# A gated recurrence and a PReLU layer on one core: two kinds of sums moved from VectorE to TensorE, factors folded, and the hand-made instruction order replaced

## The chip, the core and the metric

The kernel runs on one core of a Trainium2 chip. The core has five engines with a queue of their own: TensorE (PE; the profile shows its weight loads apart, as PEld), VectorE (DVE), ScalarE (ACT), GpSimd (POOL) and SyncE (SP), which here issues all the DMA transfers. Each engine works through its queue in order and waits on semaphores for the others. The metric is device time in microseconds (us), the median of several executions; lower is better.

## The reference

An attention block with a gated complex state feeds a dense layer. For each of 4 batches and 8 heads, over 768 tokens with head size 48:

```python
mag = np.sqrt(a_re * a_re + a_im * a_im)
scale = np.minimum(mag, 0.999) / (mag + 1e-06)
a_re_n, a_im_n = (a_re * scale, a_im * scale)
for t in range(S):
    ar, ai = (a_re_n[:, :, t, :, None], a_im_n[:, :, t, :, None])
    new_re = ar * S_re - ai * S_im
    new_im = ar * S_im + ai * S_re
    kv = np.einsum('bhd,bhe->bhde', k[:, :, t], v[:, :, t])
    S_re, S_im = (new_re + kv, new_im)
    y[:, :, t] = np.einsum('bhd,bhde->bhe', q[:, :, t], S_re)
```

The outputs, as 3072 tokens of 384 numbers, go through `h = x @ w_in` (384 to 2048), `g = max(h, 0) + alpha * min(h, 0)` and `g @ w_out` (2048 to 384). All is float32.

## The kernel before

**Units.** The 768 tokens of a batch are six units of 128, so there are 24 units, 0 to 23. A unit (`unit`) first turns queries and keys by the accumulated phase of the gates (L742, L744, on DVE), and then makes six doubling steps (L797, one DVE instruction of 96x1024 each), between which PE forms the scores of a level (L759, tile `ps_lv`) and DVE or ACT masks them (L782, L773). After the steps its keys are transposed (L868, `ps_kt`), ACT copies them beside the unit's decays in tile `T` (L870, L871), PE multiplies keys by values (L880, `ps_kv`), and the state is carried on in two halves: ACT scales the old state (L916, eight instructions, one a head) and DVE adds `ps_kv` to it (L918). PE makes the outputs from scores (L900) and from the old state (L930), ACT copies them out (L944) and two DMAs write them to DRAM (`ysc`, L949).

**Gates.** Before a unit can begin, its gates must be there. `gates` works in nine groups: group 0 has one unit, group 1 two, groups 2 to 8 three units each. ACT squares the real and the imaginary part (L263 to L267; L299 to L303 for group 0), DVE adds the squares (L269; L305), ACT and DVE make the reciprocal root and the normalised gate (L272 to L291; L310 to L323, L363), and DVE makes the decays (L380). From them a tree of ever shorter products (L396) makes the decays of whole spans, and one DMA writes all to DRAM (`decs`, L401). Then come the phases: products of unit complex numbers in several passes (L416, L418, L477, L507, L510), and two DMAs (`phs`, L512). The units load them again as `PP` (L665) and `T` (L672).

**The dense layer.** It works on ten groups of tokens, m = 0 to 9: groups 0 and 1 have one unit each, the others two. `xT` is loaded from `ysc` (L962) when the group's units are out; `features` multiplies by `w_in` (L978, `ps_h`), ACT and DVE make the PReLU (L985, L987), and `outputs` multiplies by `w_out` (L997, `ps_o`). A last group of units is done with fewer products (L1097, L1172). The weights arrive as float64 and are turned into float32 on the way (L588 to L600).

**The order.** The body is written as tasks, Python generators that yield before each instruction. `ORDER` is a string with one letter a step: it says which task goes on next, and so fixes the order of every engine's queue and of the DMAs on SP. The numbers in `yield DVE(...)` do nothing in this program. In the kernel before, the decay tree is part of the gates' task, and a unit's transposes, state and outputs are one task in a fixed sequence.

**What is where at the start.** PE's first matmul is that of unit 0's first level. The first features (m = 0) need the outputs of unit 0; from then on PE has the units and the dense layer at once.

Of the kernel before, what the change touches and what calls it, by code (L numbers as in the profile page):

```python
# [15 lines left out]
PSUM = bass.MemoryType.PSUM  # L16
DRAM = bass.MemoryType.DRAM

P = 128
# [11 lines left out]
    "AAJMMAABAJAAAAAAAAAAAAAAAAAAAAMMMBJMAAAAAAAAAAKANAOAAAABAAANAAAKANNNABAMAJNBKOAKBOOKAABMAKABAAALOAAB"  # L31
    "LAKNOLNAALBOLANNAALBBLAAKBAKBBAKABABKMAAKBAAOAABAAAAAABABBABAAABAOOABABMANAAAAAAABAAAKBABNABBNBNOBOC"
    "BOCBJNNBLBOJBBOONBBNBBOCBBPBCBPPJLJMJCLKBNBCMBCJBPLBPCBOPPJCPBBBPOBPPBBNBPBBNNBBCPPMLPBLBBPLKBPKBCCC"
    "PLOKBKBPKBBBBCBPKCOOPKBPPPCPBPBCBPPPPBBPBCBBPBBPBBPBPCBPMPBCCBCBPNBKLCCNLCNPCPOCOJDCNDPPPJCOJNNCCCNJ"
    "OCNOOLCNOPCNKOMNNCPQPDJCQDLCDNQPPDQQQLCDQDKQQMCLNDQDOKPQQMODQLOOJQJDKQJDOLCQnOJOLDDJQNJOQLQLOOoLoDDC"
    "QLoQRQoLQQLQooooQQCoQDKNJooooRoMQoQCRCCoooooQoRDQQQCODDCONNCooRQRLoDCLRoMoLoCRRLCoooooCJoRDKCRKooooo"
    "RCDoRQLCDLCoooCoRKoOLCDJCQDCCoLDCRRDDCooooooLCQCooCLCoCoCoLCLCCCLCRCCLCKOCRCRLoCooCRRRCRRoRRCoCRCQQC"
    "CRCQCCoRKCRQRQQCQOORRoRCCQCCooRRCNQDoLoDLoNoDNoooNDoEDNNoEOJoDJRJDRLoooooDDoLDRRRLDRRLRDNDNEJDJSDDRo"
    "oJDESDEDSRDRJESSnJSoLESDoLoLODJSSJDSDLLTSDJoELoooooSSSDLoLooooJSSoDDDoSEDLoooSToSoJooJSSSDoSSDSSoooo"
    "ooSTSDETooooTToSEEoEDoooooSDToSEDTSESSSSDooLDTLoooLEEDSLToLSLoooooDLELoTJDSSSDoooooTTSDSESSSLoDooooo"  # L40
    "SEEDTLLoTKoooooDDDToTEJLDDDDoooooTEUJTDKoDoooKTToDoLoToooTLoUoDJoTLToooToEJoDonooToDEoDTKoUoDJooToUo"
    "EoEUTUEoETEDDDJTooUooDoUUoDooToToTTDoLoLoULoLDULLoooUUoDoLooooDoULoLoELooooLoUULoTLUTLJoooooFUEUoETT"
    "TUUUUTTTUooooTToUETUUFEoUEooooEoUVoUEoooooVVKJJUUEUUEUUoFooLEFLoUoLEUFJVUELoVJoUJooooVJEoFVEJEVoEUoo"
    "oUUUEVoEUoLoVVLEoooEoLEoVEJooooJVEWoFEnVVLoVELoLoooEoKVVEoELVEoJFooooJWoVoVFooWLooLVVEEWoLWVoLWVEFJV"
    "VVJEooVoVoooEKoWKoJEoooVEWWooVWoVoEFWVVVEVVEWELWEELooFEELoWLEoEoLoWWLVLoWEEEEVLLooooooLWEWLEoLEFELEK"
    "FFVVVooWooLooVVVVVFFFVLXKEoEWooooooEWWEEWWJoWWJoooWoEJWoWJoFJWoEWFFWWWWoEoELoLEoJoLoEoFXEooooFooooXo"
    "ooooKXWXLXFWoXoGGXLoXooooJWoLXoLWoFWXoXWFXWoFWXFWWoWXoXFFoFLoXoGFJFnGooooXXoJFoFLoLXXXXLGFLoooooXLFX"
    "XXoGoLFGFLoooooooFXoooGFoJoYJXoJFoJXFGKoooXFYFXoXFYJFooooGXXXYoYXLYFooLXFYFKoLoYoYLXXFZLFXLoXYXFLoXX"
    "XoooYXoFGLGFYYLoYGoFJoYFYJoooFoFZoLFoJoYJGKooooFJGYFYLooYYYLoJYYZGLLFoooooZLoFGYZYZoYZYKJFZZooooYFoZ"
    "YoYFGZYYFYFFYYFZFLFZFFLoYLoooZLooLoFFFFFYFZLFZYYYLFoZLYYFLYoooFZYLaZFLoFoooZZZZoYZZLZoGYFFLLoooZoZGo"  # L50
    "LGoFZJoZFFFGJoooooFooZFFZZFZZZGLoonoFLooLaoFoLoooaJoLoZoaJGoLZooaJaGoaoHoLZZLaaZoHGGoGZGZGGaZLGaLooo"
    "ooaZGaLoaJoZaZaooooGJoHaooHGoooaoaGLaHoooLoGLaaJaHoaJaaJoooooHoGbaoaGHoooaoGaobbJKHoaGaoaoaGaaHoLKoG"
    "JoboLGobLGoLGoooGbLoHGHbLboJbHoGJLaoLbbGLooooGoGHobLGaLaHbLGbabLaabaaGoLaooooLGbboGoGHbGooooJbGbGGKo"
    "bbboJobJbGGbcbbJobGGoooboGcbooooGbGoHbGbGcbbbLGcGLoooGbLcGHcGGJoboJcoLJGGGobLGccLGoobKcbLobHLbobbLoc"
    "obHoGHGdbLGHooooccocGoJoJHoooLcocdJooLconJHLoooocLcHoccccoccLGoJdcGGooocodHocHoHdHoHcGGGcoooGooocGGc"
    "GccccodGLLoooGcodooooLoddJoooLocdoLoIHIoHLdooooLHooLHdcoLdcoLdcLocJHcocddoHoHooKcoooILdocoLHoIHdcdLH"
    "LddoIKdooooJdoIddJoddKdHoHooodoHdoIoHedHHodeHIdddodoHLeHLoLoIHodLHoHLHeIHoLdLoooeeJHeHLoLdddHoooeeoH"
    "JHdedHLoJooooeIoLIeLeoeJddoLHoooLeeoLoHdIHeodJoHIHoooeeoJeeeeoeJeoeIJeoenJHIHoooeJIoeooHeHoHfeeoeHfe"
    "eoLLHoHHJHoHHeHoLfeoLILJHHHHofLooooofeLHfeHfLeHKoeIeLoKffLeHoooooefHeoeLgIIfogJLooooIoooffofoHJILooo"
    "ooHLffoJIoJfHHoooooKHofofJooLfffffofKoJgooHofgIoooggoIHIofofHIoIIoofoHKfooHofogfffoffggoLHLoLogoLoHI"  # L60
    "oLgoooILofnoIfgLgLgLfffoLggJoLgfKoooofooooIgLogfooLfIfofggggggogoohgogIhhLJJJIIhIooooogogoIIoogggggg"
    "oLILogoJIoJgIohJgIILgIgooohLIIgoJgIoIghILhIoIghILoLhhIooooIoIhIoJoLihILJooohhohLoLohLohoooLioJIIoLho"
    "LoJiJooohohooJhhiohhihJhihnoIIIhIoIIhIIIIooohIoIhIioIhihhhhhIihoLihLLLohhhLIIIIIiooooLohhiILiIoLiILo"
    "hLoooiiIoLohihohoLIoooILiIiLoLiiiiiioJioJioIIiIoooioiojoioIiiijIiiJooLojLoJoIoJoLjoooiLoIioLojIjiiiI"
    "jiiooooojjooooLojLiiJoooojLopoLjojiiLoooJjoLoojjJLojLLoooooJojLojooJjjjjjJojjJopjojookkkoojojooojjkj"
    "jojjokLkoLkLokJokoLokLoLoookLjooLjkJkokLLokkLoooLokooooLojjjLokjkjojkjjkojkkLlkookkopkJokJpoookokook"
    "oklkkkkLkLoookJlooLoLolooJokJopoJoLllJklnkLllokoooooklolokooollkkLLLolkoololoooJoLloJoLoooLlmlololoo"
    "oloLoLlooolLmooomololloolpmooolomlomopoomoomomoooomooomoollllllmmomoolomomoooolmoonoolllmmomlmomlmol"
    "lomomoooooooomLooLooooLoLoooLoooooooLoqLoooLooLomLooooLooLooLomLoooooooopooooomoooomoooooooooooooooo"
    "oooooooomomomoomoomomoooomomomoqlmqlmqmmmqqmqoooooqqoqoooooqoqqoqooqoqqooqoqqoqoqooqooqqoooooqoqqoqo"  # L70
    "ooooooooooqoooqoooqqoqqoqooooooooooqqooqoooooqqoqqoqooqoqooqoqqoqqqqqqqqoooooooooooqoqqoqoqooqooqooq"
    "oqoqooqoqoqoooqqqoqqonoooooooooooooooqooqqoqoqqoqqooooooooooooqqoqoqoooqooooooooooooqqqooqooqoooqoqq"
    "oqooooooooqqoooooooooqoooooooooooqooqoooqqoooqoqqqoqooooooooqoqoooqoqooooqqoqqoqooqoqooqqqoqoqqqqqqq"
    "ooooqoooooooqoqqoqooqqqoqoqooooooooooooqqqqqqoqqoooooooooooooooooqqqqoqqoqqooooooooooooooooooqoqqqoq"
    "oqoooooooooooooooooqqooooooooooooqoooqoqoooqoqqoqqoooooooooooqqqooooooqoqqoqqooqoqooqoqqqqqooooooooo"
    "ooqoqqoqooqoqooqqoqqqqqqqqqqqqqqqqqqqqqqqqq")


class Ring:

    def __init__(self, n):
        self.n = n

    def put(self, event, i=None):
        pass


class Plan:

    LETTERS = "ABCDEFGHIJKLMNOPQRSTUVWXYZabcdefghijklmnopqrstuvwxyz0123456789"  # L90
# [12 lines left out]

@with_exitstack
def kernel(
# [123 lines left out]
    def gates(g, b, c0, c1):  # L229
# [111 lines left out]
        def by_place(z):  # L341
            return z.rearrange("p (n m i) -> p m n i", m=L // 2, i=2)

# [917 lines left out]
```

## Time and profile before

| | |
|---|---|
| median of 3 runs | 823.86 us (821.32, 823.86, 829.38) |
| the profiled execution | 820.38 us, its span 818.6 us |
| busy in the span: PE | 681.1 us (83%) |
| DVE | 693.9 us (85%) |
| ACT | 520.3 us (64%) |
| POOL | 222.2 us (27%) |
| DMA | 130.99 MB, mean 160 GB/s |
| first matmul | at 54.1 us |
| first features of m = 0, 1, 2, 3 (L978) | at 120.1, 184.1, 220.3, 266.2 us |

The busy times add up to far more than the span, since the engines work side by side. What counts is which of them waits for which at each stage; the prediction shows the profile by stage.

### The profile page before, as it was taken

The numbers are of one execution on the slowest core, as the hardware profiler recorded it, in microseconds if no ns is written. First come the engines' busy times: TensorE is split into PE (matmuls) and PEld (weight loads), VectorE is DVE, ScalarE is ACT, GpSimd is POOL, SyncE is SP. The second block draws the span as 40 slices with busy tenths as digits, with TensorE's granted clock in tenths as the row PEclk, the third lists the DMA queues.
The fourth block names the chain that finished last, engine by engine and source line by source line (L and its number), as shares of the span: only waits on it lengthen the run. The fifth ranks groups of instructions, "written<-read, shape, count | busy, mean of one in ns | idle before, by whom it ended". The sixth has DMA issues, their size and how long they took to land.

```text
span 818.6 us, 27870 instructions
## 1 busy us (share of the span) xinstructions
PE 681.1 (83%) x11680; PEld 539.0 (66%) x11680; DVE 693.9 (85%) x1191; ACT 520.3 (64%) x1307; POOL 222.2 (27%) x293
## 2 busy tenths in 40 slices
PE   0003128659998999999999999999999999999997
PEld 0003126537776777767777777777777777899997
DVE  5999999999989899999999989998787775456574
ACT  8777998669666777876876697555756544312121
POOL 7231343051604310531245054003200000233342
PEclk9999659979999999999999999999999999999999
DMA  8594895593689589738865867787566622101000
GB/s 242 176 294 128 266 296 158 177 253 101 182 235 197 140 194 272 174 90 279 195 168 141 253 160 180 223 197 184 117 182 134 153 77 56 44 1 40 1 21 20
DMA packets 186598, 130.99 MB, mean 160 GB/s; under 512 B 74728, under 2 KB 176872, under 8 KB 186088
## 3 DMA queue, kind: packets, MB, share of 16 engines
q1 hardware_dynamic: 186472, 129.20, 59.3%
q8 instruction: 92, 1.51, 0.8%
q14 instruction: 34, 0.28, 0.1%
HBM read 100.82 MB, written 35.71 MB: 167 GB/s over the span
## 4 chain that ended last, share of the span: by engine, by line
PE 65%; DVE 14%; DMA 10%; ACT 4%; SPq 2%; issue 2%; POOL 1%; DVEq 0%; ACTq 0%; POOLq 0%
PE ps_o L997 19%; PE ps_h L978 18%; PE ps_m L1172 7%; PE ps_lv L759 5%; PE ps_y L1097 4%; PE ps_h L1097 4%; PE ps_y L900 3%; DVE KQ L797 2%; PE ps_kv L880 2%; PE ps_y L930 2%; DMA VL<-in_v_dram 2%; DVE gate L507 2%; PE ps_kt L868 1%; DVE gate L416 1%; DMA T<-decs 1%
## 5 line engine op out<-in xcount | busy, mean ns | idle before, releaser
L978 PE MATMUL ps_h<-xT,w_in_sb 128*128 128x256 f32 (+1 forms) x960 | 227.0, 369 | 2.1 <-DVE w_in_sb L600 1.6
L997 PE MATMUL ps_o<-w_out_sb,g_sb 128*128 128x384 f32 x576 | 222.1, 501 | 4.8 <-DVE g_sb L987 4.7
L978 PEld LDWEIGHTS ps_h<-xT,w_in_sb 128*128 128x128 f32 x960 | 170.9, 195 | 51.3 <-DVE w_in_sb L600 2.2
L797 DVE TENSOR_TENSOR KQ<-KQ,T 96x1024 f32<-96x1024 f32 x120 | 148.4, 1237 | 25.8 <-PE ps_lv L759 19.2
L997 PEld LDWEIGHTS ps_o<-w_out_sb,g_sb 128*128 128x128 f32 x576 | 102.5, 191 | 44.9 <-DVE g_sb L987 6.5
L985 ACT ACTIVATE g_sb<-ps_h 128x256 f32<-128x256 f32 (+1 forms) x160 | 57.9, 362 | 73.0 <-PE ps_h L978 72.2
L759 PE MATMUL ps_lv<-WQ 96*32 96x32 f32 x2304 | 34.4, 203 | 83.6 <-DVE WQ L742 70.2
L759 PEld LDWEIGHTS ps_lv<-WQ 96*32 96x32 f32 x2304 | 26.3, 116 | 105.9 <-DVE WQ L742 71.0
L916 ACT ACTIVATE St<-St,T 96x48 f32<-96x48 f32 x352 | 84.0, 325 | 4.6 <-DVE St L918 4.3
L987 DVE SCALAR_TENSOR_TENSOR g_sb<-g_sb,al,ps_h 128x256 f32<-128x256 f32 (+1 forms) x160 | 71.3, 446 | 13.7 <-ACT g_sb L985 13.1
L1160 POOL TENSOR_TENSOR sums<-g_sb 128x128 f32<-128x128 f32 x48 | 21.8, 475 | 185.5 <-DMA VL<-in_v_dram 110.6
L416 POOL TENSOR_TENSOR gate<-gate 128x72 f32<-128x72 f32 x42 | 34.5, 822 | 133.7 <-ACT gate L446 130.9
L596 POOL TENSOR_SCALAR top<-top 128x768 f32<-128x768 f32 x16 | 44.1, 2755 | 74.6 <-ACT top L588 63.2
L820 ACT COPY WQ<-KQ 96x1024 f32<-96x1024 f32 x48 | 50.0, 1041 | 18.9 <-DVE KQ L797 18.3
L416 DVE TENSOR_TENSOR gate<-gate 128x576 f32<-128x576 f32 (+5 forms) x84 | 50.7, 604 | 1.1
L900 PE MATMUL ps_y<-A,VL 64*48 64x64 f32 x2304 | 41.9, 220 | 4.4 <-issue 4.3
L900 PEld LDWEIGHTS ps_y<-A,VL 64*48 64x48 f32 x2304 | 39.0, 122 | 6.8 <-issue 6.7
L507 DVE TENSOR_TENSOR gate<-gate 128x1152 f32<-128x1152 f32 (+2 forms) x36 | 42.8, 1220 | 0.8 <-POOL gate L492 0.7
L1135 ACT ACTIVATE rl<-g_sb 128x256 f32<-128x256 f32 x24 | 10.0, 416 | 50.0 <-DVE g_sb L1128 50.0
L773 ACT ACTIVATE A<-ps_lv,columns 128x64 f32<-128x64 f32 x144 | 37.4, 336 | 6.2 <-PE ps_lv L759 5.9
L836 ACT COPY W<-KQ 96x512 f32<-96x512 f32 x48 | 30.8, 641 | 16.2 <-DVE KQ L797 8.7
L759 PE MATMUL ps_lv<-KQ,W 96*32 96x32 f32 x1536 | 24.7, 204 | 18.5 <-ACT W L836 17.4
(168 smaller groups left out, 1355.7 us busy)
## 6 DMA issues: line engine op xcount, KB each, us to landing
T<-decs SPq DMA_DIRECT2D x48, 384.0 KB
PP<-phs SPq DMA_DIRECT2D x24, 387.0 KB
KQ<-in_q_dram SPq DMA_DIRECT2D x48, 192.0 KB
decs<-gate SPq DMA_DIRECT2D x7, 1152.0 KB
phs<-gate SPq DMA_DIRECT2D x14, 576.0 KB
KQ<-in_k_dram SPq DMA_DIRECT2D x40, 192.0 KB
vsc<-in_v_dram SPq DMA_DIRECT2D x48, 144.0 KB
VL<-vsc SPq DMA_DIRECT2D x48, 144.0 KB
```

What stands on the lines that cost most here:

```text
L416: on(4 * k).tensor_tensor(out=m, in0=w[:, 1::-1].unsqueeze(2).to_broadcast([P, 2, 2, k]), in1=pairs_of(u), op=ALU.mult)
L507: TT(out=m[:, a], in0=U5[:, 1 + a], in1=turned(off3, o)[:, a].unsqueeze(1).unsqueeze(3).to_broadcast([P, L // 2, nb, 2]), op=ALU.mult)
L759: nc.tensor.matmul(t[64 * i + j:64 * i + j + HC // 2, p], lhsT=keys(n, g), rhs=queries(n, g), start=True, stop=True)
L797: nc.vector.tensor_tensor(out=x, in0=x if x0 is None else x0, in1=m, op=ALU.mult)
L900: nc.tensor.matmul(o, lhsT=Vp[h][64 * i:64 * i + 64, s, e_ * D:(e_ + 1) * D], rhs=a, start=False, stop=False)
L916: nc.scalar.activation(St[:, n], before[:, n], AF.Copy, scale=T[0:D2, n, TL - 4 + s:TL - 3 + s])
L978: nc.tensor.matmul(p, lhsT=w_in_sb[:, f // 2, kk, f % 2 * P:(f % 2 + 1) * P], rhs=x_of[m][:, kk], start=(kk == 0), stop=(kk == NK - 1))
L985: nc.scalar.activation(gt, p, AF.Relu, scale=-1.0)
L987: nc.vector.scalar_tensor_tensor(out=gt, in0=gt, scalar=al_1[:, f:f + 1], in1=p, op0=ALU.mult, op1=ALU.add)
L997: nc.tensor.matmul(sums[0], lhsT=gt[:, c * P:(c + 1) * P], rhs=w_out_sb[:, f], start=(f == 0), stop=(f == NF - 1))
L1097: nc.tensor.matmul(o, lhsT=lhs, rhs=rhs, start=(at in (0, 5)), stop=(at in (4, 8)))
L1172: nc.tensor.matmul(banks[k][:, half], lhsT=lhs, rhs=rhs, start=(j == 0 and half == 0), stop=(j == NF // 2 - 1 and at in (2, 3, 5, 6)))
```

## The change

1. *The first gates' squares.* In groups 0, 1 and 2 the two squares are added by PE: two matmuls with the identity as weights, summed in PSUM (`sum_of_squares`, tiles `ps_h`, `ps_y`, `ps_o`), and the instructions that read the sum read it from PSUM, in three parts for group 2.
2. *The first six units' state.* For units 0 to 5 the scaled state is added to keys by values on PE: one matmul with the identity starts the sum in PSUM, the products of keys and values go on top of it, and ACT copies the sum back. DVE's addition is left out there.
3. *Factors folded.* The scale of 2^16 is put into the first instruction, the signs and halves into others. The rescaling of `c` on ACT goes, and the product of `x` with its factor is written by DVE straight into the place of the unit numbers, so that ACT copies only `y` and its negative.
4. *Tasks of their own.* The decay tree with its DMA (`decay_tree`) and each unit's transposes and state (`unit_state`) become tasks, which `ORDER` can place freely.
5. *`ORDER` is a new string.*

```diff
+SUMMED = 3
+EARLY = 6
...
+    def sum_of_squares(z, a, b_):
+
+        for i in range(z.shape[1] if len(z.shape) > 2 else 1):
+            parts_ = [x[:, i] if len(z.shape) > 2 else x for x in (z, a, b_)]
+            for j in range(2):
+                nc.tensor.matmul(parts_[0], lhsT=ident, rhs=parts_[1 + j], start=j == 0, stop=j == 1)
...
-        x, c, f, d, e, y = [G[:, i] for i in range(6)]
+        f, e, x, d, y, c = [G[:, i] for i in range(6)]
...
-            nc.scalar.activation(x, x, AF.Identity, scale=1.5, bias=bias_tiny)
+            nc.scalar.activation(x, x, AF.Identity, scale=1.5 * GATE_SCALE, bias=bias_tiny)
             yield ACT(N)
-            nc.scalar.activation(c, x, AF.Square, scale=GATE_SCALE)
+            nc.scalar.activation(c, x, AF.Square)
...
-            t = yield DVE(N, t)
-            TT(out=c, in0=c, in1=d, op=ALU.add)
+            if g < SUMMED:
+                banks = {1: ["y"], 2: ["h", "h", "o"]}[g]
+                t = yield PE(4 * N * 1.68e-3, t, takes=[R[z] for z in banks])
+                sums_ = bank_views(banks, N)
+                for z, row in sums_:
+                    sum_of_squares(z, row(c), row(d))
+            else:
+                t = yield DVE(N, t)
+                TT(out=c, in0=c, in1=d, op=ALU.add)
+                sums_ = [(c, lambda row: row)]
...
-            TT(out=e, in0=e, in1=c, op=ALU.mult)
+            for z, row in sums_:
+                STT(out=row(e), in0=row(e), scalar=-1.0, in1=z, op0=ALU.mult, op1=ALU.mult)
...
-            TT(out=c, in0=c, in1=d, op=ALU.mult)
-            ts = yield ACT(N, ts)
-            nc.scalar.activation(c, c, AF.Copy, scale=1.0 / (1.5 * GATE_SCALE))
+            for z, row in sums_:
+                TT(out=row(c), in0=z, in1=row(d), op=ALU.mult)
...
-            for o, p in ((2, y), (1, x)):
-                tu = yield ACT(N, tx, *after)
-                nc.scalar.copy(U5[:, o], by_place(p))
-            tu = yield ACT(N)
+            if C < 3:
+                yield ACT(N, ty)
+                nc.scalar.copy(U5[:, 2], by_place(y))
+            tu = yield ACT(N, *after)
             nc.scalar.activation(U[:, 0], U[:, 2], AF.Copy, scale=-1.0)
...
-            for p, w in ((x, -0.5), (y, -0.75)):
-                tx = yield DVE(N, t)
-                STT(out=p, in0=p, scalar=w * GATE_SCALE, in1=d, op0=ALU.mult, op1=ALU.mult)
+            ty = yield DVE(N, t)
+            STT(out=y, in0=y, scalar=1.5 * GATE_SCALE, in1=d, op0=ALU.mult, op1=ALU.mult)
+            tx = yield DVE(N, t)
+            TT(out=U5[:, 1], in0=by_place(x), in1=by_place(d), op=ALU.mult)
+            if C > 2:
+                ti = yield ACT(N, ty, tx)
+                nc.scalar.copy(U5[:, 2], by_place(y))
...
+    def decay_tree(g, b, c0, c1):
...
+            (tiny_engine if k <= SMALL else nc.vector).tensor_tensor(
+                out=dec[:, :, at + m:at + m + m // 2], in0=pairs[:, :, :, 0], in1=pairs[:, :, :, 1], op=ALU.mult)
+            at += m
+        t = yield DMA(NK * C * P, t)
+        nc.sync.dma_start(scr_of[b * NCH + c0][0].rearrange("(t p) c s -> p t (c s)", p=P),
+                          dec.rearrange("p (t c) s -> p t (c s)", t=NK))
...
+    def unit_state(u):
...
+        for s in range(1 if last else 2):
+            k_ = yield ACT(5 * H * D, states[s][1] if s else ("state", u - 1) if c else ("begun", u), takes=(R["St"],))
...
+            for n in range(H):
+                nc.scalar.activation(St[:, n], before[:, n], AF.Copy, scale=T[0:D2, n, TL - 4 + s:TL - 3 + s])
+            if u < EARLY:
+                bank = "lv" if s else "misc"
+                k_ = yield PE(1.2, k_, e, ("V", u), takes=(R[bank],), mode=2, n=17)
+                V = L["V"]
+                sum_ = ps.tile([P, H, D], F32, tag=bank, name="ps_kv", bufs=2 if s else 1)
+                nc.tensor.matmul(sum_.rearrange("p n d -> p (n d)"), lhsT=ident[0:D2], rhs=St.rearrange("p n d -> p (n d)"),
+                                 start=True, stop=False)
+                keys_by_values(sum_, s, True)
...
+                k_ = yield ACT(H * D, k_)
+                nc.scalar.copy(St, sum_[0:D2])
+            else:
+                k_ = yield DVE(H * D, ek, k_)
+                nc.vector.tensor_tensor(out=St, in0=St, in1=kv[s][0:D2], op=ALU.add)
...
+        for u in range(NU):
+            plan.add(unit_state(u))
+        for i, g in enumerate(GATES):
+            plan.add(decay_tree(i, *g))
         plan.run(ORDER)
```

Group 0's two halves are changed in the same way as the groups 1 and 2. Units 6 to 23 keep DVE's addition.

More of the change, by code (lines that the diff above doesn't have):

```diff
@@ L79 @@
+    "qqqqqqqqqqqqqqqqqqqqqqqqqqqqq")
 class Ring:
@@ L863, in unit @@
         last = c + 1 == NCH
[L864 to L882 removed]
+        done["stepped", u] = k_
+        T, V = L["T"], None
         for s in range(2):
@@ L901, in unit @@
                                              rhs=a, start=False, stop=False)
[L902 removed]
+        for name in (1, 4, 16, 32):
             R[name].put(ev)
[L904 to L923 removed]
+        v_used(u, ev)
         g, cg = group_of[u]
         for s in range(2):
[L927 to L928 removed]
+            e = yield PE(0.47, q_, ("known", u, s), mode=1, n=8)
+            before = before_of[u][s][0]
             for n in range(H):
```

305 lines of the change are left out of this document (167 added, 138 removed).

## The prediction, made before the changed kernel was run

> **What bounds the kernel now.** I began with the busy strip of the page, then took the stages one by one, then the chain of waits at their borders, and last the groups by shape for prices.
>
> The strip: each digit is the busy share, in tenths, of a fortieth of the span (20.5 us).
>
> ```profile
> PE   0003128659998999999999999999999999999997
> DVE  5999999999989899999999989998787775456574
> ACT  8777998669666777876876697555756544312121
> PEclk9999659979999999999999999999999999999999
> ```
>
> DVE is full from the second slice on, PE from about the tenth. So the kernel has a first part, in which DVE sets the pace and PE is mostly idle, and a second, in which PE sets it. The same by stages that end at the first features (L978) of m = 0, 1, 2, 3; the columns are the stretch, its length, busy time of PE, PEld, DVE, ACT and POOL with counts, granted clock, DMA share, GB/s:
>
> ```profile
> 0.00:54.00 54.00, 0.00 (x0) 0.00 (x0) 42.94 (x118) 41.52 (x71) 23.81 (x36) 1.00 0.80 225
> 54.00:120.00 66.00, 15.53 (x588) 13.07 (x588) 64.71 (x101) 56.40 (x87) 17.27 (x8) 0.75 0.84 244
> 120.00:184.00 64.00, 44.53 (x870) 34.45 (x860) 62.56 (x110) 46.73 (x115) 23.46 (x18) 0.86 0.71 194
> 184.00:220.00 36.00, 33.90 (x753) 27.04 (x752) 35.39 (x63) 28.65 (x80) 13.67 (x16) 1.00 0.51 139
> 220.00:266.00 46.00, 43.41 (x726) 33.12 (x724) 41.44 (x58) 30.72 (x77) 10.55 (x15) 1.00 0.82 210
> 266.00:400.00 134.00, 131.30 (x2424) 98.31 (x2428) 126.71 (x184) 103.95 (x269) 32.33 (x36) 1.00 0.74 195
> 400.00:540.00 140.00, 138.72 (x2583) 103.53 (x2573) 130.54 (x186) 100.69 (x264) 46.75 (x50) 1.00 0.71 184
> 540.00:710.00 170.00, 169.48 (x3049) 127.73 (x3049) 130.72 (x210) 89.86 (x284) 18.90 (x37) 1.00 0.52 127
> ```
>
> PE's idle time is 54.0, 50.5 and 19.5 us in the first three stages, 2.1 and 2.6 in the next two, and 4.5 us in the last three together: 128.7 of its 137.5 us lie ahead of 266 us. DVE idles 1.3 and 1.4 us between 54 and 184. Only an earlier full PE, or less work on PE behind that point, shortens this kernel. The chain of waits (start, us, what) shows what else stands in the first part, and where it goes over to PE:
>
> ```profile
> 91.51 6.21 DMA gate<-in_a_im_dram
> 97.73 9.52 DMA KQ<-in_k_dram
> ...
> 260.53 5.60 DMA xT<-ysc
> 266.17 1.56 PE ps_h L978 x6
> ```
>
> Transfers are on the path at 91 to 107 us; from 266.17 us on the chain is almost wholly PE.
>
> **The change, part by part.** Times are the rows' mean durations; positions come from the order in which each program puts its instructions on an engine.
>
> *Squares on PE.* DVE loses two L305 (0.36 each), one L269 of 128x768 (0.95) and one of 128x1152 (1.37): 3.0 us. Group 2's two readers come in three parts: three 128x384 (0.55, as L507 has it) for 1.37, twice, gives 0.6 back. PE gets ten matmuls of 384 columns (0.65, a pair of L997 passes in the chain) and four of 192 (0.33): 7.8 us, all ahead of its first matmul at 54.1 us, so under 54 us of idle time. If that cover were gone they would cost 7.8. On group 0's path ACT, PE, ACT takes the place of ACT, DVE, ACT: 0.66 for a half's two matmuls against 0.36. I take +0.3, bounds 0 and +1.
>
> Here the clock matters. The keys by values of unit 0 took 1.96 us at 79 us, where the clock is low, and those of unit 1 took 1.08 us at 127.9. [...]
>
> *States on PE.* Units 0 to 5 have eleven L918 (0.547): 6.0 us off DVE. ACT gets eleven copies (0.48, as L870): 5.3 us. PE gets eleven matmuls of 384 columns: 7.2 us, and the products of a half now run alone, not beside those of the other half; bounds 0 and 1.3 times a unit's kv of 1.0 us, I take 2.8 in all. Seven to eight of the eleven come before 184 us, under 19.5 us of idle time; units 4 and 5 pay some 3 us on a full PE.
>
> *Factors.* ACT loses the rescaling of c (L291: 0.83, seven of 1.16, 0.52 in group 0) and a copy of x (L355: 0.87, seven of 1.27; 0.7 in group 0): 20 us. DVE keeps its count; the strided product costs what L510, strided too, costs (1.35 against 1.38 for L363). With the copies of the states ACT's queue goes from 520.3 to 506.2 us. ACT is never the fullest engine, so I count this at 0; bounds 0 and -2, since DVE's L987 waited 13.1 us for L985 in all. New is that a group's decays (L380) wait for ACT's copy of y; behind them stand the tree and the phases. Ten or more DVE instructions lie between, so 0.
>
> *Trees and states as tasks.* DVE's sum is the same, but the order moves. In group 2 the busy time of DVE between the last product of the tree and the first L507, which overwrites the decays and so waits for their DMA, falls from 56.5 to 6.2 us. That DMA has 1152 KB. The `phs` transfers, half as large, held the chain 4.53 and 4.23 us; twice that is 9 us, and at the 330 GB/s of 100 to 120 us it is 3.5. So the wait is 0 to 2.8 us, and behind it on DVE stand group 2's phases, which unit 3 waits for. I take 1. On SP the `decs` of groups 1 and 2 go from places 43 and 86 to 68 and 127, past unit 0's loads and the first `xT`. That can only help those; it is a rival below.
>
> *The sum.* I add up what stands ahead of a point on DVE, each at its row's mean. Ahead of the first L987 of m = 1: 171.7 us before, 166.5 after. Ahead of the last step of unit 5: 220.4 and 213.9. PE, with each matmul at its mean distance to the next start, has 619.8 us behind the first feature of m = 1 before and 624.5 after; behind that of m = 3 543.2 and 542.4. (These prices add up to 2% less than PE's busy time; only differences are used.)
>
> - m = 1 begins at 184.1 - 5.1 = 179.0.
> - m = 3 begins, as PE has it, after 82.1 us more (624.5 - 542.4): 261.1, if it never waits. Before, 76.6 us of work took 82.1. As DVE has it, at 266.2 - 6.5 = 259.7. I take the later one and 1 us of waits: 262.1, so -4.1.
> - Behind m = 3: -0.8, the same waits. Group 2's DMA +1, group 0's path +0.3.
>
> That is -3.6 us: 816.8 against the profiled execution's 820.38 (span 818.6), 820.3 against the median. The profile lies just below the three runs, so I put **818 us**, a gain of 0.4 to 0.7%. A difference under 1% is about what a measurement of this kernel can't tell from none.
>
> **The rivals.**
>
> *The start comes earlier still (faster).* 1152 KB leave the stretch of 91 to 121 us, where the chain stands on transfers for 27 us, and 768 KB leave the way of the first `PP`, which took 6.69 us. At 330 and 289 GB/s that is 3.5 and 2.7 us. For it: DMA shares of 0.79 and 1.10 in 80 to 120 us. Against: DVE was full there anyway, so the transfers hid behind other work of DVE. If all of it comes through: -3.6 - 6.2 = -9.8, some 811 us.
>
> *The gain is eaten by PE (no change).* At m = 1 PE has 4.7 us more behind it than before, nearly the 5.1 that DVE gains. If the waits between m = 1 and m = 3 (5.5 us) stay as they were, m = 3 begins at 266.6 and nothing is won: 820 to 824. For it: units 4 and 5. Against: those waits were for DVE and `xT`, which come earlier.
>
> *States hold PE (slower).* A state's sum stands in PE's in-order queue and waits for eight ACT instructions (1.8 us), before it does its own 0.65. Behind it stand other units' levels and features, which DVE waits for. Before, PE met a state only at L930, and once stood 5.28 us. If each of the nine sums of units 1 to 5 stops PE for 2.4 us, that is 21.6; the first stages' idle time hides some, yet DVE's steps slip with PE's levels. It decides against the change from about 1.3 us a sum net of cover; with 13 to 17 lost, 830 to 834 us. Against: the ACT work ahead of these sums is 3 to 6 us less than it was ahead of L916.
>
> **How the numbers follow.** The forecast (-1 to -8 us) gets 0.44, the earlier start 0.27, the eaten gain 0.16, the held PE 0.13. Above 1% faster lie the earlier start and 0.05 of the forecast: 0.32. Slower by over 1% is the held PE: 0.13. The rest, 0.55, is within 1%. The range, 806 to 829: below, the earlier start with ACT's 2 us and the 2.5 us by which the lowest run lies under the median; above, the eaten gain with the 5 us by which one run of three lies over the median. It leaves out most of the held PE.
>
> **What would show it.** DVE's busy time about 8 us less, ACT's 14 less, PE's about 18 more. The first features of m = 1 near 179 us and of m = 3 near 262, with the distance from there to the end unchanged at 552 us. A wait of DVE before group 2's first L507 of 0 to 3 us. If m = 3 begins early but the end doesn't follow, I have misjudged what bounds the second part; if PE waits for ACT before the states' sums, the third rival is at work.

## The result and the profile after

| | before | changed |
|---|---|---|
| median (range), 4 runs each on the same chip | 825.35 us (821.32 to 829.38) | 835.15 us (833.18 to 838.88) |
| ratio, 95% interval | | 1.0133 [1.0091, 1.0176] |
| the profiled execution, its span | 820.38, 818.6 us | 834.42, 832.6 us |
| busy PE, DVE, ACT | 681.1, 693.9, 520.3 us | 718.1, 685.8, 506.0 us |
| first features of m = 0, 1, 2, 3 | 120.1, 184.1, 220.3, 266.2 us | 112.7, 184.2, 220.7, 269.3 us |
| from m = 3 to the end | 552.4 us | 563.3 us |

The change made the kernel 1.3% slower, 835 us against a predicted 818, outside the predicted range of 806 to 829. Of the 14.0 us between the two spans, 3.1 are there when m = 3 begins, and 10.9 come behind it. The busy strips of the page of the changed kernel, to be held against those of before:

```profile
PE   3043459649999999999999999989999999999997
...
DVE  5999999979988998989898999978785686556573
...
PEclk8565559779999999999999999999999999999999
```

PE has work from the first slice on; DVE has a gap in its ninth slice, at 167 to 187 us, where it was full before. The clock rows can't be compared ahead of some 83 us: the first clock record of the trace of before lies at 82.9 us, and the row counts as full ahead of it. The matmuls tell more: the first levels (`ps_lv<-WQ`) took 241 ns a pass between 62 and 80 us in both kernels, and 196 ns behind 125 us. So PE ran slowly there before, too. The same stretches as the prediction's (length, busy time of PE, PEld, DVE, ACT, POOL with counts, granted clock, DMA share, GB/s):

```profile
0.00:54.00 54.00, 12.53 (x24) 7.32 (x25) 42.80 (x116) 40.64 (x68) 24.76 (x37) 0.65 0.77 218
54.00:120.00 66.00, 26.75 (x610) 20.10 (x609) 64.45 (x103) 55.73 (x91) 20.63 (x8) 0.55 0.88 247
120.00:184.00 64.00, 46.88 (x850) 35.65 (x848) 55.64 (x103) 43.15 (x114) 19.81 (x22) 0.82 0.65 169
184.00:220.00 36.00, 34.17 (x665) 27.02 (x663) 34.07 (x58) 28.13 (x82) 4.94 (x8) 1.00 0.62 174
220.00:266.00 46.00, 46.00 (x755) 35.27 (x756) 41.10 (x58) 30.21 (x77) 9.39 (x17) 1.00 0.72 188
266.00:400.00 134.00, 130.02 (x2470) 95.96 (x2472) 122.30 (x176) 96.06 (x255) 25.31 (x36) 1.00 0.74 193
400.00:540.00 140.00, 138.57 (x2555) 102.97 (x2545) 129.61 (x185) 95.57 (x257) 36.76 (x47) 1.00 0.69 183
540.00:710.00 170.00, 165.06 (x2908) 123.81 (x2907) 126.72 (x195) 90.06 (x278) 15.94 (x28) 0.99 0.55 139
```

Two places stand out. From 120 to 184 us DVE idles 8.4 us instead of 1.4, so what it was relieved of became idle time. And from 540 to 710 us PE, which set the pace there, idles 4.9 us instead of 0.5.

**Where m = 1 is held.** Two lines of DVE's timeline before (start, us, engine, line, operation, tiles and shapes): the last product of group 2's phases, and the first turn of unit 3, which needs them back from DRAM.

```profile
157.31 1.36 DVE L510 TENSOR_TENSOR gate<-gate 128x1152 f32<-128x1152 f32 x1
172.44 1.22 DVE L742 TENSOR_TENSOR WQ<-KQ,PP 96x1024 f32<-96x1024 f32 x1
```

The same two in the changed kernel; the bracket is the idle time of DVE just before:

```profile
157.78 1.36 DVE L540 TENSOR_TENSOR gate<-gate 128x1152 f32<-128x1152 f32 x1
172.48 1.34 DVE L795 TENSOR_TENSOR WQ<-KQ,PP 96x1024 f32<-96x1024 f32 x1 [2.58 <-DMA T<-decs]
```

The pair has not moved. Ahead of that product DVE is busy for 141.9 us instead of 143.9, and it waited 15.9 us there instead of 13.4. Everything else that DVE lost stood behind the product, where DVE now waits for the transfers. The view names `T`, but the turn reads `KQ` and `PP`, and by the trace's semaphores `PP`, issued at 163.8 us, landed at 172.4. Before, it was issued at 163.5 and landed at 170.0, while DVE had work of its own up to the turn. So without DVE's work the turn could have come 2.4 us earlier at most, and the slower load took just that; why it took 8.6 us instead of 6.6 stays open. PE's queue has unit 3's first level ahead of m = 1: it starts at 173.9 us (173.7 before), and m = 1 some 10 us later in both. In the changed kernel m = 1 has a second bound, its `xT`. SP issues that load at 177.71 us (before at 174.95), behind loads of `V` and `PP`, and PE's weight loads wait for it:

```profile
184.09 0.76 PEld L1070 LDWEIGHTS ps_h<-xT,w_in_sb 128*128 128x128 f32 x6 [0.33 <-DMA xT<-ysc]
```

**What PE waits for behind m = 3.** PE's waits from m = 3 to the end, before (line, releaser: us in total, times, longest); "issue" names no releaser:

```profile
PE ps_y L900 <- issue: 3.9, 4, 1.3
PE ps_h L978 <- DMA xT<-ysc: 0.5, 1, 0.5
PE ps_kt L868 <- ACT T L871: 0.2, 1, 0.2
```

The same in the changed kernel:

```profile
PE ps_lv L812 <- ACT W L890: 5.8, 8, 2.8
PE ps_y L937 <- issue: 1.3, 1, 1.3
PE ps_h L1070 <- DMA xT<-ysc: 0.9, 1, 0.9
PE ps_kt L990 <- DVE KQ L850: 0.9, 1, 0.9
...
```

Before, PE waited 0.7 us for others there; now 8.7 us (all such waits of the view together), most of it a unit's next level (L812) that waits until ACT has copied that level's keys into `W` (L890). The copy itself waits for DVE: ahead of the longest of these waits, which ends at 562.61 us, ACT had waited 4.69 us for DVE's step (L850), that step 1.42 us for `T`, and the unit's first turn 3.36 us for `PP`. The stops at "issue" went the other way, from 3.9 to 1.3 us.

### The profile page after: what moved, and what is told of

It reads as the page before. It is cut to its first block, busy times and chain, and to the rows that moved or that the text cites. A ratio compares the mean times of both kernels' runs of the same rounds, so it can differ in the third digit from the quotient of the medians.

```text
span 832.6 us, 27905 instructions
## 1 busy us (share of the span) xinstructions
PE 718.1 (86%) x11730; PEld 560.6 (67%) x11730; DVE 685.8 (82%) x1180; ACT 506.0 (61%) x1301; POOL 198.6 (24%) x293
## 3 DMA queue, kind: packets, MB, share of 16 engines
q8 instruction: 92, 1.51, 0.8%
## 4 chain that ended last, share of the span: by engine, by line
PE 54%; DVE 14%; DMA 13%; ACT 8%; SPq 6%; issue 3%; POOL 1%; DVEq 0%; ACTq 0%
PE ps_o L1089 13%; PE ps_h L1070 13%; PE ps_m L1264 6%; DVE KQ L850 4%; DMA PP<-phs 4%; PE ps_h L1189 4%; PE ps_y L1189 3%; PE ps_lv L812 3%; PE ps_y L937 3%; DMA T<-decs 2%; PE ps_y L947 2%; SPq L757 2%; DMA ysc<-T 2%; PE ps_kv L999 1%; DMA V<-in_v_dram 1%
## 5 line engine op out<-in xcount | busy, mean ns | idle before, releaser
L1070 PE MATMUL ps_h<-xT,w_in_sb 128*128 128x256 f32 (+1 forms) x960 | 228.1, 368 | 4.5 <-DMA xT<-ysc 4.4
L1070 PEld LDWEIGHTS ps_h<-xT,w_in_sb 128*128 128x128 f32 x960 | 171.4, 193 | 57.1 <-DMA xT<-ysc 4.0
L850 DVE TENSOR_TENSOR KQ<-KQ,T 96x1024 f32<-96x1024 f32 x120 | 147.4, 1228 | 27.4 <-PE ps_lv L812 16.8
L446 POOL TENSOR_TENSOR gate<-gate 128x72 f32<-128x72 f32 x42 | 20.5, 488 | 145.7 <-ACT gate L476 110.6
L812 PEld LDWEIGHTS ps_lv<-WQ 96*32 96x32 f32 x2304 | 26.1, 115 | 39.5 <-ACT WQ L874 11.5
L890 ACT COPY W<-KQ 96x512 f32<-96x512 f32 x48 | 30.8, 642 | 33.6 <-DVE KQ L850 31.2
L812 PE MATMUL ps_lv<-WQ 96*32 96x32 f32 x2304 | 34.2, 202 | 18.1 <-ACT WQ L874 11.1
L937 PE MATMUL ps_y<-A,VL 64*48 64x64 f32 x2304 | 45.0, 225 | 1.6 <-issue 1.3
L812 PE MATMUL ps_lv<-KQ,W 96*32 96x32 f32 x1536 | 24.2, 203 | 23.6 <-ACT W L890 23.6
L937 PEld LDWEIGHTS ps_y<-A,VL 64*48 64x48 f32 x2304 | 41.0, 126 | 3.6 <-issue 2.8
L795 DVE TENSOR_TENSOR WQ<-KQ,PP 96x1024 f32<-96x1024 f32 x24 | 30.7, 1279 | 14.8 <-DMA PP<-phs 10.0
L245 PE MATMUL ps_h<-gate,ident 128*128 128x192 f32 (+1 forms) x16 | 8.4, 705 | 38.6 <-ACT gate L291 34.2
```

Source lines behind the costliest of these rows:

```text
L446: on(4 * k).tensor_tensor(out=m, in0=w[:, 1::-1].unsqueeze(2).to_broadcast([P, 2, 2, k]), in1=pairs_of(u), op=ALU.mult)
L812: nc.tensor.matmul(t[64 * i + j:64 * i + j + HC // 2, p], lhsT=keys(n, g), rhs=queries(n, g), start=True, stop=True)
L850: nc.vector.tensor_tensor(out=x, in0=x if x0 is None else x0, in1=m, op=ALU.mult)
L937: nc.tensor.matmul(o, lhsT=Vp[h][64 * i:64 * i + 64, s, e_ * D:(e_ + 1) * D], rhs=a, start=False, stop=False)
L1070: nc.tensor.matmul(p, lhsT=w_in_sb[:, f // 2, kk, f % 2 * P:(f % 2 + 1) * P], rhs=x_of[m][:, kk], start=(kk == 0), stop=(kk == NK - 1))
```

## The experiments

The theory after the result: the new order costs the time, and the sums on PE are about neutral. Rivals: the sums hold PE's queue; the squares' low clock does; a transfer is issued too late.

**One part at a time.** Four kernels. *old_order_squares* is the kernel before with the changed kernel's gates (squares on PE, factors folded) and the old order, the tree in its old place. *old_order_all_parts* has the states on PE too; there the old state comes last:

```diff
+            if u < EARLY:
+                nc.tensor.matmul(kv[s].rearrange("p n d -> p (n d)"), lhsT=ident[0:D2], rhs=St.rearrange("p n d -> p (n d)"),
+                                 start=False, stop=True)
+                nc.scalar.copy(St, kv[s][0:D2])
+            else:
+                nc.vector.tensor_tensor(out=St, in0=St, in1=kv[s][0:D2], op=ALU.add)
-            nc.vector.tensor_tensor(out=St, in0=St, in1=kv[s][0:D2], op=ALU.add)
```

*new_order_state_dve* is the changed kernel with the states' sums on DVE again, and *new_order_all_dve* has the squares' there too (so it keeps the order, the tasks and the folded factors):

```diff
-                nc.tensor.matmul(sum_.rearrange("p n d -> p (n d)"), lhsT=ident[0:D2], rhs=St.rearrange("p n d -> p (n d)"),
-                                 start=True, stop=False)
-                keys_by_values(sum_, s, True)
+                keys_by_values(sum_, s, False)
...
-                nc.scalar.copy(St, sum_[0:D2])
+                nc.vector.tensor_tensor(out=St, in0=St, in1=sum_[0:D2], op=ALU.add)
```

> The kernel before with its own order of steps; only the gates are those of the changed kernel: the squares of groups 0, 1 and 2 added by TensorE, and the factors folded (the steps that this leaves empty stay in the order as empty steps). State sums stay on VectorE. Theory A (the new order loses the time): 815 to 824 us, at or a little below the kernel before (825), since VectorE has 2.4 us less and ScalarE 20 us less. Theory B (the squares on TensorE lower its clock or stop it): 828 us or more.

> As the run with the old order and the squares, and the state sums of units 0 to 5 on TensorE too: the products of keys and values stay at their old place in the queue on top of a bank set to zero by one more matmul, the scaled state is added there by one matmul with the identity, and ScalarE copies the sum. So all computing parts of the change are there, with the old order. Theory A (order): 815 to 826 us. Theory B (the state sums hold TensorE's queue, as the 6.13 us wait before such a sum at 155.9 us of the changed kernel shows): 5 us or more above the run with the squares alone, 830 us or more.

> The changed kernel with its order, but the states of units 0 to 5 added by VectorE again: keys by values at the place of the sum on TensorE, without the matmul of the state, and VectorE's addition at the step of ScalarE's copy. Theory A (order): 832 to 838 us, as the changed kernel (835). Theory B (state sums hold TensorE): the waits of TensorE for the scaled state (3.0, 6.4 us) go and the time falls by 5 us or more, to 830 us or less.

> The changed kernel with its order, with both the states and the first gates' squares added by VectorE; what is left of the change is the folded factors, the tasks of their own and the new order. Theory A (order): 832 to 840 us, VectorE's 8 us more to do in the first part adding up to 4. Theory B (sums on TensorE): 826 us or less.

Measured: 852.06 us (851.25 to 853.01), 848.75 (847.27 to 854.34), 843.46 (835.30 to 845.94) and 853.69 (849.05 to 856.12), against 822.76 of the kernel before. All four are slower than the changed kernel, also those that undo a part of it, so no sum over parts can be made of them. What three of them share is a number that none of the theories had: PE stops behind m = 3 of 17.2, 15.8, 3.8 and 16.3 us at "issue", against 3.9 before. Counted along PE's queue, these stops lie at like places: nearly all at remainders 191 to 195 of the count modulo 256 (a float32 matmul is four instructions, two weight loads and two passes: the four of group 0's squares are eight of each in the trace). The page of the changed kernel, like that of before, has a DMA queue for the instructions (packets, MB, share):

```profile
q8 instruction: 92, 1.51, 0.8%
```

92 packets in 1.51 MB are 16 KB each. PE's 11680 weight loads and 11680 matmuls of the kernel before come to 254 a packet, so I take a packet for a block of PE's queue. Then each edit that adds matmuls ahead shifts the places of all later ones.

**The count of PE's instructions.** The kernel before gets tiny float32 matmuls at the head of its queue, where PE has nothing else to do: *before_14_dummies* shifts it by 56 instructions, as the fourteen of the squares do, and *before_64_dummies* by 256.

```diff
+        first = ps.tile([P, DM], F32, tag="h", name="ps_first", bufs=2)
+        for _ in range(14):
+            nc.tensor.matmul(first[:, 0:1], lhsT=ident, rhs=ident[:, 0:1], start=True, stop=True)
```

*changed_32_dummies* gives the changed kernel another 128. *changed_v_later* moves the loads of `V` and `VL` (letter `L` of `ORDER`) behind the next ready loads of phases and decays at twelve places.

> The kernel before, with 14 matmuls of one column put at the head of TensorE's queue (its first real matmul comes only at 54 us, so they lie in idle time); nothing else is changed. Four instructions each: 56, as the squares add in the run with the old order. Theory F (TensorE runs dry of instructions where its queue passes places 256 instructions apart, as all stalls of the old-order runs lie at the same remainder of 256; a shift moves these places into other work): 835 to 852 us. Rival (the order of buffers and waits alone counts): 822 to 826, as before (823 to 825).

> The same with 64 such matmuls, 256 instructions: the places at which the queue can run dry fall on the same instructions as before. Theory F: within 4 us of the kernel before (821 to 829). Rival (extra instructions as such cost time): above the run with 14.

> The changed kernel with 32 such matmuls at the head of TensorE's queue (128 instructions), nothing else. Theory F: another set of stalls, so a time that differs from the changed kernel's 835 by more than 4 us in either direction. Rival: 834 to 837.

> The changed kernel with one edit in the order: where the load of V waited for keys by values by over 1.5 us and held SyncE's queue, the load of V and the part of the VL loads behind it go behind the next transfers that were ready (the decays, the phases, PP, the outputs), in 12 places. Theory S (SyncE's queue, blocked by V for 70 us in all against 39 before, delivers PP and T late, for which VectorE waits 18 us behind 190 us against 3): 825 to 831 us. Rival (TensorE's own work and stalls): 833 to 838.

Measured, against 822.69 us: 842.44 us (841.13 to 843.56), ratio 1.0230 [1.0206, 1.0254]; 824.57 (819.48 to 830.61), 1.0023 [0.9998, 1.0049]; 863.94 (859.17 to 868.43); 841.93 (841.55 to 842.33). Fourteen matmuls in idle time cost 19.8 us, sixty-four nothing that can be told: it is the remainder that counts. A stop in the timeline of *before_14_dummies*:

```profile
401.98 1.51 PE L900 MATMUL ps_y<-A,VL 64*48 64x64 f32 x87
406.19 0.46 PE L900 MATMUL ps_y<-A,VL 64*48 64x64 f32 x7 [2.70 <-issue]
406.59 2.93 PE L997 MATMUL ps_o<-w_out_sb,g_sb 128*128 128x384 f32 x4
```

Amid a run of small matmuls PE stands for 2.70 us, and then does four outputs in 2.93 us that take 2.0 at its row's mean (507 ns each). Two windows of the same kernel, ahead of the stop and behind it, show the second cost (the column of 1.00 and 0.51 is the granted clock):

```profile
400.00:403.50 3.50, 3.49 (x130) 2.94 (x128) 3.50 (x6) 3.50 (x12) 0.00 (x0) 1.00 1.08 248
406.10:409.50 3.40, 3.31 (x12) 1.95 (x13) 0.55 (x1) 0.15 (x1) 0.00 (x0) 0.51 0.12 32
```

*changed_32_dummies* differs from the changed kernel as expected, but for two reasons. Its 32 matmuls at the head took 13.8 us (0.43 each) and held group 0's squares, so that m = 0 came at 123.5 us instead of 112.7; its first part says nothing of remainders. Behind m = 3 the stops rose from 1.3 to 15.1 us. *changed_v_later* missed: with `V` loaded later, DVE's waits for phases and decays did not get shorter.

**The same remainder.** So parts were compared again with dummies that give PE's queue, behind the first groups, the remainder of the kernel before (*old_order_all_aligned*, 33 dummies) or of the changed kernel (*new_order_state_dve_aligned*, 11; *new_order_all_dve_aligned*, 25). *old_order_factors* needs none: it has the old order and the folded factors, its squares are on DVE, and PE's queue is as before:

```diff
+SUMMED = 0
...
+            if g < SUMMED:
...
+            else:
+                t = yield DVE(N, t)
+                TT(out=c, in0=c, in1=d, op=ALU.add)
```

> The kernel before with its own order, only the factors folded in all nine groups (20 us less on ScalarE, steps left empty where instructions go); squares and states stay on VectorE, and TensorE's queue is the same instruction for instruction. Theory F (the second part is set by TensorE's queue: its order and where it runs dry): 818 to 825 us, as the kernel before (822.7) or up to 4 less. Rival (the folded factors themselves cost the time, by the new wait of the decays for a copy): 830 or more.

> The run with the old order and all computing parts (849 us), with 33 matmuls of one column at the head of TensorE's queue, so that its queue from unit 6 on lies at the same remainder of 256 instructions as in the kernel before. Theory F: its stalls behind 270 us fall from 15.8 to about 4 us, and with the slow clock behind them the time falls to 824 to 834; what is left above the kernel before comes from the first part, where the squares hold TensorE's queue (unit 0 began 4 us later). Rival (sums on TensorE cost it): 845 or more.

> The run with the new order and the states added by VectorE (843 us), with 11 matmuls of one column at the head of TensorE's queue in place of the 11 taken away: from unit 6 on the queue lies as in the changed kernel. Theory F: the distance from the first features of m = 3 to the end comes back from 570 to 563 us. If the state sums themselves cost nothing net, 833 to 838 us; if their waits on TensorE (6.1 us at unit 2) set m = 1, 828 to 832.

> The run with the new order and both sums on VectorE (854 us), with 25 such matmuls in place of the 25 taken away. Theory F: from 578 to about 563 us behind the first features of m = 3, 832 to 840 in all, so the sums on TensorE bring or cost less than 5 us, and the new order alone is what loses against the kernel before. Rival: the sums on TensorE are worth their 8 us of VectorE: 842 or more.

Measured, against 821.94 us: 826.47 us (825.06 to 829.52), 1.0044 [1.0018, 1.0071]; 849.04 (842.32 to 852.89); 835.42 (830.96 to 840.21), 1.0135 [1.0065, 1.0204]; 833.78 (831.27 to 839.11), 1.0141 [1.0079, 1.0204]. *old_order_all_aligned* missed: its dummies took 14.24 us at the head and held the squares, as above. *old_order_factors* lies between its two theories. At the changed kernel's remainder no worth of its sums on PE shows, either way: ratios of 1.0133 with all of them, 1.0135 without the states', 1.0141 without any; the intervals reach some 3.5 to 6 us to each side, so less than that can't be told. The squares don't bring PE's slow pace between 54 and 120 us (the granted clock is 0.55 there in the changed kernel). The matmuls of m = 0 with them (L1070, changed kernel) and without them (L1069, *new_order_all_dve_aligned*), in ns a pass (least, median, most):

```profile
L1070 PE MATMUL ps_h<-xT,w_in_sb x12: 421/422/582, 112.7 to 117.5; 128*128 128x128 f32 x12
L1069 PE MATMUL ps_h<-xT,w_in_sb x12: 421/421/582, 112.6 to 118.5; 128*128 128x128 f32 x12
```

Behind 125 us the median is 275 ns in both. What a full clock there would be worth, no run shows.

**The old order behind a seam.** *new_order_to_m3_then_old* keeps the changed kernel with its `ORDER` up to the first features of m = 3, and has the rest in the sequence of the kernel before; *new_order_to_m1_then_old* has its seam at m = 1. *old_order_squares_aligned* repeats the first experiment at the right remainder. In these three the dummies (39, 39, 50) stand behind group 1's squares and give the rest of the queue the remainder of the kernel before:

```diff
+                if g == 1:
+                    first = ps.tile([P, DM], F32, tag="h", name="ps_first", bufs=2)
+                    for _ in range(39):
+                        nc.tensor.matmul(first[:, 0:1], lhsT=ident, rhs=ident[:, 0:1], start=True, stop=True)
```

There they write column 0 of a bank of PSUM that still holds the first half of group 0's sums, so those 128 values are not the reference's; the instructions and their sizes are the same. *before_58_dummies* shifts the kernel before by 232 instructions, where, by the positions of its bursts, fewer stops were expected.

> The changed kernel with all its parts; its own order up to the first features of m = 3, and from there the steps still to do in the order of the kernel before. 39 matmuls of one column behind group 1's squares (TensorE idles there) put TensorE's queue at the same remainder of 256 as in the kernel before. Theory O (the new order of the second part loses the 11 us behind m = 3): m = 3 near 269, 552 to 556 us from there to the end, 822 to 827 in all. Rival (the second part loses by what the first part leaves late, or by the parts): 832 or more.

> The same with the new order only up to the first features of m = 1. Theory O: 820 to 828, near the run with the new order up to m = 3, since m = 1 begins at the same 184 us in both kernels. Rival (TensorE's queue of the new order between m = 1 and m = 3 is what costs): 4 us or more below the run up to m = 3.

> The run with the old order, the squares on TensorE and the factors folded (852 us), with 50 matmuls of one column behind group 1's squares, where TensorE idles, so that from there on its queue lies at the same remainder of 256 as in the kernel before. Theory F: behind m = 3 back from 576 to 552 to 557 us; with the first part as in that run (m = 3 at 273.6, from unit 0's late start) 826 to 833. Rival: 842 or more.

> The kernel before with 58 matmuls of one column at the head of TensorE's queue: 232 instructions, a remainder 24 instructions below its own. Worked out from the trace of before (places 256 apart, 320 instructions from the request to the place, the measured delays of the loads), this remainder loses some 3 us less to stalls than its own: 818 to 823 us, at or just below the kernel before on the same chip. Rival: no difference from the run with 64.

Measured, against 822.58 us: 834.34 us (832.91 to 834.58), 1.0143 [1.0101, 1.0185]; 848.96 (844.02 to 850.27); 829.05 (827.88 to 831.59), 1.0077 [1.0042, 1.0112], where the same program without dummies took 852.06; and 837.00 (836.58 to 839.18), 1.0177 [1.0127, 1.0227], a miss. Neither seam made a faster kernel: the theory that the new order alone costs the time had 822 to 827 us for the first and 820 to 828 for the second, so both missed. The rival of the first, that the second part loses by what the first leaves late or by the parts, had 832 or more, and this is the number that came out; what its traces say against it stands below. The first lost right behind it, at 279 to 304 us, where stops of up to 3.7 us lie; the second reached m = 3 only at 283.2 us.

**All traces on one scale.** From each trace the distance from m = 3 to the end, less PE's stops at places of the instruction queue and less half of its time at the low clock (granted 0.50 in the changed kernel; both behind m = 3), is what is left to the order. The last column is what PE waits there for other engines and transfers.

| kernel | order behind m = 3 | m = 3 begins | to the end | stops | low clock | left | waits for others |
|---|---|---|---|---|---|---|---|
| before | old | 266.2 | 552.4 | 3.9 | 0 | 548.5 | 0.7 |
| before_14_dummies | old | 267.3 | 572.1 | 19.6 | 6.8 | 549.1 | 0.2 |
| before_58_dummies | old | 267.4 | 570.1 | 15.0 | 10.2 | 550.0 | 1.9 |
| before_64_dummies | old | 266.8 | 556.3 | 7.7 | 0 | 548.6 | 0.4 |
| old_order_factors | old | 268.1 | 555.8 | 4.4 | 0 | 551.4 | 2.7 |
| old_order_squares | old | 273.6 | 575.9 | 17.2 | 13.7 | 551.8 | 2.8 |
| old_order_squares_aligned | old | 273.0 | 553.7 | 2.5 | 0 | 551.2 | 2.2 |
| old_order_all_parts | old | 275.2 | 572.2 | 15.8 | 10.2 | 551.3 | 1.9 |
| old_order_all_aligned | old | 287.8 | 563.0 | 6.5 | 10.2 | 551.4 | 2.5 |
| new_order_to_m3_then_old | old | 270.4 | 562.5 | 9.3 | 6.8 | 549.8 | 1.7 |
| new_order_to_m1_then_old | old | 283.2 | 559.1 | 6.7 | 3.4 | 550.7 | 1.6 |
| changed | new | 269.3 | 563.3 | 1.3 | 3.4 | 560.3 | 8.7 |
| new_order_state_dve | new | 272.3 | 570.4 | 3.8 | 13.1 | 560.0 | 8.7 |
| new_order_state_dve_aligned | new | 270.7 | 567.8 | 0.7 | 10.2 | 562.0 | 10.6 |
| new_order_all_dve | new | 269.1 | 578.1 | 16.3 | 10.2 | 556.7 | 5.1 |
| new_order_all_dve_aligned | new | 269.3 | 560.2 | 1.9 | 3.4 | 556.6 | 5.7 |
| changed_32_dummies | new | 276.6 | 580.9 | 15.1 | 17.0 | 557.3 | 6.2 |
| changed_v_later | new | 270.6 | 570.0 | 3.4 | 10.2 | 561.5 | 10.1 |

The raw distances overlap (552 to 576 us with the old order, 560 to 581 with the new), which is why the first set could not be read. What is left does not: 548.5 to 551.8 with the old order, whatever else is in the kernel, and 556.6 to 562.0 with the new one. The waits for others go along with it, 0.2 to 2.8 against 5.1 to 10.6 us. These are single profiled executions, and the split is worked out, at half the length of the slow stretches; but the gap of some 5 us holds over eighteen traces, and in the two with a seam the same program changes sides where its order does. That the order costs the time behind m = 3 rests on this split, not on a faster kernel.

**Which wait of the new order.** The phases of groups 4 to 8 end 0.9, 7.4, 7.4, 7.2 and 9.5 us later in the changed kernel than before. Two more kernels move the letters of these gates and their trees (`E` to `I`) earlier behind m = 3, by 40 and 100 places, with PE's queue unchanged.

> The changed kernel with one edit in the order, behind the first features of m = 3 alone: all steps of the gates of groups 4 to 8 and of their decay trees stand 40 steps of the order earlier (some 7 us); TensorE's queue stays the same, instruction for instruction. Theory G (the groups' last phases end 7 to 9 us later than before from group 5 on, so PP and T come late, VectorE waits 16 us for transfers behind m = 3 and TensorE stops for it, with the slow clock behind one such stop): VectorE's waits for PP fall from 8 to under 3 us, 827 to 832 us in all. Rival (VectorE's own work is what comes late; gates put earlier push the units' steps back): 834 or more.

> The same with 100 steps (some 17 us). Theory G: no wait for PP left, 825 to 832 us. Rival: 836 or more, above the run with 40.

Measured, against 823.09 us: 876.56 us (871.80 to 883.43) and 888.16 (887.06 to 889.30), much slower. The waits of PE in the first of them, from m = 3 on:

```profile
PE ps_kt L991 <- DVE KQ L851: 9.2, 4, 2.6
PE ps_lv L813 <- ACT W L891: 7.2, 4, 3.0
PE ps_lv L813 <- DVE KQ L851: 4.5, 4, 1.9
```

Gates that come earlier push a unit's steps back on DVE, and PE waits for those. Earlier phases are no cure, at least not moved all together. Which step of the new order would have to move, for PE not to wait for the copies into `W`, stays open, and so does what the new order would take at other remainders than the four that ran. No kernel here was faster than the one before.

## Why the prediction was wrong, point by point

- *DVE 8 us less, ACT 14 less, m = 0 earlier, group 2's wait 0 to 3 us.* Right: 8.1 and 14.3 us less, m = 0 at 112.7 instead of 120.1, and the wait of group 2's first product for the tree's DMA was 0.8 us. (The terms given for ACT come to 505.7 us, not 506.2.)
- *PE about 18 us more.* It was 37, of which 23.8 lie ahead of 120 us. The squares took 14.3 us (2.90, 4.35, 5.49 and 1.55), not 7.8: they were priced at PE's pace at a granted clock of 1.00, 0.65 us a matmul of 384 columns. Group 2's first four, at 0.50, took 1.37 us each; its last two, from 54.00 us on and nearly all at 1.00, took 0.78. PE idled most of that time before, and without the sums on PE the end came no earlier (ratio 1.0141).
- *Group 0's squares.* The four matmuls of its two halves, eight passes, in the timeline of the changed kernel:

```profile
4.37 2.90 PE L245 MATMUL ps_h<-gate,ident 128*128 128x192 f32 x8 [4.37 <-ACT gate L340]
```

  They took 1.45 us a half, not 0.66. The first clock record of this trace comes only at 13.2 us, so what clock they had is not shown. A later result did not follow: unit 0's first turn (L795) began at 50.3 us, before at 52.9.
- *"m = 1 begins at 184.1 - 5.1 = 179.0."* **The first step that failed.** I added up all DVE work ahead of m = 1's first L987, as if m = 1 waited for DVE's sum. In PE's queue unit 3's first level stands ahead of it, and that level's turn on DVE needs group 2's last phase product back from DRAM. Ahead of that product DVE was busy for only 2.0 us less, and it waited 2.5 us longer; behind it `PP` landed 2.4 us later than before. With these sums back on DVE, in *new_order_all_dve_aligned*, m = 1 began at 184.9 us, after a wait of 1.24 us for `xT`, which the new order issues later. So in the new order transfers hold m = 1, and not DVE's sum.
- *"m = 3 begins, as PE has it, after 82.1 us more."* It was 85.1, and 84.4 with no sums on PE, so most of this is the order's, not the states' products.
- *"Behind m = 3: -0.8, the same waits."* **The step that cost most.** The sum of PE's work behind m = 3 says nothing of the order it is done in. The distance grew by 10.9 us: 11.8 of what is left to the order, 1.7 of low clock, less 2.6 of stops. Of the 11.8, waits for others make 8.0 (8.7 against 0.7); the rest is not placed. I took an order of several thousand letters as equal because its totals were equal.
- *Factors at 0, bounds 0 and -2.* Alone in the old order they cost 4.5 us by the medians (826.47 against 821.94; by the interval 1.5 to 5.8), though the prices came out about as worked out: the strided product took 1.42 us, and ACT was busy 18.7 us less. PE's waits for ACT's copies into `W` rose from 0 to 1.6 us behind m = 3; the rest is not placed. From there to *new_order_all_dve_aligned*, another 7.3 us (833.78) go with the new order and its tasks, at another remainder; what is left to the order is 551.4 us in the one and 556.6 in the other.
- *The rival "states hold PE".* The mechanism is there. Two of PE's waits at 120 to 184 us in the changed kernel:

```profile
PE ps_kv L1030 <- ACT St L1024: 6.4, 2, 6.1
PE ps_lv L812 <- DVE WQ L795: 6.3, 1, 6.3
```

  and in the chain of waits, where that stop of 6.1 us ends at 155.91 and the granted clock is 0.50 from 153.2 to 163.4 us:

```profile
153.94 1.92 ACT St L1024 x8
155.91 1.65 PE ps_kv L1030 x2
157.56 1.66 PE ps_kv L999 x27
```

  No price of it shows: 835.42 us (830.96 to 840.21) with the states on DVE. PE stood there, but what came next, unit 3, waited for its phases anyway. So this rival named the side that came out, by a mechanism that did not bring it about.
- *"The gain is eaten by PE"* was nearest up to m = 3 (266.6 predicted, 269.3 measured), and it too kept the second part as it was.
- *The range* left out that the second part could get longer by its order, and that any edit to PE's queue shifts the places at which it stops. The changed kernel was lucky in that: 1.3 us of stops. Several of the experiments lost 15 to 20.

## What to carry to other kernels

Take work off an engine only after asking which of its instructions the next stage waits for: what is queued behind that one becomes idle time, not an earlier stage. Where a change replaces a whole instruction order, equal sums of work say little, and the forecast needs a range for the order itself, on the slow side too. Where PE runs bursts of small matmuls, compare edits at the same count of PE's instructions modulo 256, or a few matmuls in idle time can move the end by more than the edit does: here fourteen moved it by 19.8 us.

## What the runs showed of the hardware

**Stops of PE at blocks of 256 instructions.** In twenty traces, from 270 to 800 us, PE has 190 stops of over 0.5 us; 97 of them lie at remainders 191 to 195 of the count of its instructions modulo 256. Of these 97, 96 end 1.21 to 1.73 us (median 1.42) after a block of the instruction queue has come in; of the other 93, only 2 do. That is a correlation, but *before_14_dummies* and *before_64_dummies* make it a cause: 56 instructions cost 19.8 us, 256 nothing that can be told (ratio 1.0023 [0.9998, 1.0049]). The size fits the page's 92 packets of 16 KB, at 254 of PE's weight loads and matmuls a packet. In *before_14_dummies* such stops add up to 19.6 us behind m = 3, in the changed kernel to 1.3.

**The clock fell after some short stops.** A line of the changed kernel's timeline, at the end of its longest wait behind m = 3:

```profile
562.61 0.58 PE L812 MATMUL ps_lv<-KQ,W 96*32 96x32 f32 x32 [2.85 <-ACT W L890]
```

From 562.8 to 566.2 us, 3.4 us, the granted clock is 0.50, and it is 1.00 ahead of it (552 to 562.6) and behind it. After a stop of 2.70 us in *before_14_dummies* it was 0.51 (406.1 to 409.5 us), after one of 2.66 us in *old_order_squares* 0.50 (414.6 to 417). After one of 3.1 us in *before_14_dummies* it stayed at 1.00 (486.1 to 490). So the length of a stop alone does not tell whether the clock falls.

**Matmuls of one column are not free.** In *old_order_all_aligned* thirty-three of them, 66 passes, took 14.24 us at the head of the queue, 0.43 each, and held the matmuls behind them: group 0's squares began at 15.75 us, in *old_order_all_parts* without them at 4.45.
